# Eight one-row writes of the lead, issued by ScalarE's queue in place of SyncE's

## The chip, the cores and the metric

The kernel runs on one core of a Trainium2 chip. The metric is device time in microseconds (us) of one execution; lower is better. TensorE, VectorE, ScalarE and GpSimd are called PE, DVE, ACT and POOL in the profile, as there; SP is SyncE, which only issues DMAs, and SPq and ACTq are DMA issues by SyncE and ScalarE.

## What is computed

A linear attention with a complex decay (4 batches, 8 heads, 768 positions, 48 dimensions per head), and behind it two feed-forward layers over the 3072 tokens. Cut to what matters, the reference is

```python
mag = np.sqrt(a_re * a_re + a_im * a_im)
scale = np.minimum(mag, 0.999) / (mag + 1e-06)
a_re_n, a_im_n = a_re * scale, a_im * scale
for t in range(S):
    new_re = ar * S_re - ai * S_im
    new_im = ar * S_im + ai * S_re
    S_re, S_im = new_re + kv, new_im              # kv = k[t] outer v[t]
    y[:, :, t] = np.einsum('bhd,bhde->bhe', q[:, :, t], S_re)
h = x @ w_in                                      # x: y as 3072 x 384
sp = np.where(h > 20.0, h, np.log1p(np.exp(np.minimum(h, 20.0))))
x2 = (h * np.tanh(sp)) @ w_out                    # d_ff 2048
out = ((x2 @ w_a) * (x2 @ w_b)) @ w_out2          # d_ff 1536
```

## The kernel before, in words

The 768 positions are cut into 6 chunks of 128, and a chunk of one batch is one unit c (24 of them, `chunk(c)` gives chunk number j and batch b, so units 0 to 3 are the first chunk of the four batches). For a unit the logarithm of the decay's size and its angle are summed over the 128 positions by a matmul with a triangle of ones (`running_sum`, L299). The sum of the logarithms gives two factors, `ep` and `em`, both halves of one tile named `size` (`decay_exp`, L319); the sum of the angles, in turns, is reduced to a fraction of a turn in the tile `a` (`reduce_angle`, L325). `scale_qk` (L356) multiplies q and k by the factors, `trig` (L361) writes cosine and sine, and `rotate_one` (L367) makes from them the rotated `qh` and `kh`, which PE transposes (`transposed`, L376), ScalarE copies out (`transposed_out`, L385) and PE multiplies to scores (`scored_in`, L401). `values` (L416) multiplies the scores with v.

Of each sum the last row (1 x 384 numbers, 1.5 KB) goes on to the next chunk of the same batch by way of memory: `hand_end` (L340) writes the last row of `ep` to `end_d`, and `hand_turn` (L335) the last row of the reduced angle to `turn_d`. `read_end` (L345) reads `end_d` back as the tile `g`, and `carry` (L278) reads `turn_d` for the next chunk.

The first four units are the **lead** (`lead_in`, L796): an order written out by hand as a list of step names (L841), kept on DVE, ACT, PE and POOL by added dependencies (`in_order`, L781), while SyncE's DMAs stand where the program's scheduler puts them. In this list "ep0" to "ep3" are `decay_exp` with `hand_end`, "red0" to "red3" `reduce_angle` with `hand_turn`, "at" the arctangent, "sin" `trig`, "rq" and "rk" the two rotations, "pt" and "pl" the two running sums, and "d1", "d2" the decoding of the first two weight pieces. In the lead `trig` writes cosine and sine into the tile `size` of the same unit, whose first half `hand_end` has to have read by then:

```python
t = st["turn", c]
w = st["turn", c] = st["size", c] if c < B else t
act(out=w[:, 0], in_=t[:, 0], func=AF.Sin, scale=SIN_SCALE)
```

SyncE issues the loads of a, q, k and v (192 KB each) and of the weights (768 KB a piece, `load_weights`, L140). In the built program each DMA takes the next of eight completion counters and is issued only once the DMA that had that counter before has landed.

Behind the lead, block by block of 512 tokens, follow the first layer (`moe1_h`, `mish_factor`, `mish_product`, `moe1_x2`), with the attention of the later chunks in slots between its steps, and then the second layer.

Of the kernel before, what the change touches and what calls it, by code (L numbers as in the profile page):

```python
# [21 lines left out]
def kernel(  # L22
# [14 lines left out]
    nc = tc.nc  # L37
# [31 lines left out]
    C = 128  # L69
# [34 lines left out]
    end_d = [dram.tile([1, H, D], F32, name=f"end_d{b}") for b in range(B)]  # L104
    turn_d = [dram.tile([1, H, D], F32, name=f"turn_d{b}") for b in range(B)]
    good_d = dram.tile([1, P], F32, name="good_d")

    def chunk(c):


        return divmod(c, B)
# [94 lines left out]
    st = {}  # L206
# [128 lines left out]
    def hand_turn(c):  # L335
        j, b = chunk(c)
        if j < NC - 1:
            nc.sync.dma_start(out=turn_d[b], in_=st["turn", c][C - 1:C, 0])

    def hand_end(c):  # L340
        j, b = chunk(c)
        if j < NC - 1:
            nc.sync.dma_start(out=end_d[b], in_=st["ep", c][C - 1:C])

    def read_end(c):  # L345
        j, b = chunk(c)
# [166 lines left out]
    def slot_0(c):  # L513
# [5 lines left out]
        (3, split_ell),  # L519
        (4, carry), (4, split_theta), (4, sum_ell), (5, sum_theta), (5, decay_exp), (6, reduce_angle),  # L520
        (6, hand_turn), (6, hand_end), (7, scale_qk), (10, trig),
    ]
    late = [
# [191 lines left out]
    def judge(pool):  # L715
# [20 lines left out]
        out=csum, in_=csum, pattern=[[1, P]], compare_op=ALU.is_ge, fill=0.0, base=0, channel_multiplier=-1  # L736
# [59 lines left out]
    def lead_in():  # L796
# [20 lines left out]
        def reduced(c):  # L817
            reduce_angle(c)
            hand_turn(c)

        def sizes(c):
            decay_exp(c)
            hand_end(c)
# [93 lines left out]
    for ui in range(len(units) + lag):  # L917
        if ui < len(units):
            b, f = units[ui]
# [202 lines left out]
```

## Time and profile before

| | |
|---|---|
| median of 3 runs | 1114.57 us (1113.7 to 1117.06) |
| profiled execution, its own time | 1116.88 us |
| its span, first to last instruction | 1115.2 us |
| PE, DVE, ACT, POOL busy | 95%, 59%, 55%, 21% of the span |
| mean granted TensorE clock | 0.983 of full speed |
| memory read and written | 72.44 MB and 17.36 MB |

The profile is of one execution. Busy shares are means over stages with different limits, so they tell little of any one stage; the lead takes about the first 62 us of 1115, and its instructions are read one by one in the timeline, where brackets behind a row give the idle time of its engine before it and what ended it.

### The profile page before, as it was taken

Reading aid. Unit: us, or ns where it says so; the run is one execution under the profiler, and the core shown is the slowest. Engines: PE = TensorE matmul, PEld = TensorE weight load, DVE = VectorE, ACT = ScalarE, POOL = GpSimd, SP = SyncE. Lnnn points to the kernel's source line nnn. Section 1 sums busy time; section 2 is a strip of 40 time slices with the busy share of each in tenths; the row PEclk is TensorE's granted clock in tenths of the full one; section 3 lists DMA queues with packets and bytes.
Section 4 is the critical chain, followed back from the end, with each engine's and each line's share of the span. In section 5 each row is a group of like instructions: output and inputs, shape, how many; then the busy total and the mean of one; then the engine's idle time right before and its main releaser. Section 6 shows DMA issues by size and latency. Waiting matters only on the chain.

```text
span 1115.2 us, 15205 instructions
## 1 busy us (share of the span) xinstructions
PE 1062.9 (95%) x5740; PEld 885.4 (79%) x5740; DVE 654.2 (59%) x998; ACT 615.7 (55%) x968; POOL 229.8 (21%) x220
## 2 busy tenths in 40 slices
PE   3799989999999999999999999999999999999997
PEld 1776666787888788878877878888888888888886
DVE  5699975687777677667659999742232322322222
ACT  6769877887888887779766863221121222221211
POOL 2011252444343334333332122200000000000000
PEclk9799999999999999989999999999999999999999
DMA  9445853253344443333226457310010000100000
GB/s 200 77 136 166 210 152 64 63 109 70 82 92 84 90 97 65 65 64 93 65 83 201 133 177 222 121 57 1 14 44 1 29 29 1 43 1 1 29 1 31
DMA packets 203545, 90.87 MB, mean 81 GB/s; under 512 B 144781, under 2 KB 187850, under 8 KB 203466
## 3 DMA queue, kind: packets, MB, share of 16 engines
q1 hardware_dynamic: 202426, 89.64, 32.0%
q8 instruction: 47, 0.77, 0.3%
q10 hardware_dynamic: 1040, 0.20, 0.1%
q14 instruction: 32, 0.26, 0.1%
HBM read 72.44 MB, written 17.36 MB: 81 GB/s over the span
## 4 chain that ended last, share of the span: by engine, by line
PE 56%; ACT 10%; DVE 8%; issue 3%; DMA 2%; POOL 1%; SPq 0%; ACTq 0%; POOLq 0%
PE ops L683 14%; PE psa L658 13%; PE psb L658 13%; PE hps L560 6%; PE x2ps L603 6%; ACT m L59 5%; DVE m L566 1%; DVE kh L370 1%; PE psc L404 1%; ACT L54 1%; PE py L434 1%; DVE m L580 1%; ACT s L59 1%; ACT a L59 1%; ACT r L59 1%
## 5 line engine op out<-in xcount | busy, mean ns | idle before, releaser
L669 DVE TENSOR_TENSOR a_sb<-a_sb,psb 128x512 f32<-128x512 f32 x72 | 49.4, 686 | 224.4 <-PE psb L658 224.4
L59 ACT ACTIVATE m<-m 128x512 f32<-128x512 f32 x192 | 119.4, 627 | 77.3 <-DVE m L566 73.5
L59 ACT ACTIVATE a_sb<-psa 128x512 f32<-128x512 f32 x72 | 43.0, 597 | 162.7 <-PE psa L658 160.6
L59 ACT ACTIVATE ph<-a_sb 128x512 fp32r<-128x512 f32 x72 | 45.4, 631 | 156.0 <-DVE a_sb L669 156.0
L560 PE MATMUL hps<-xh,winh 128*128 128x512 f32 x288 | 120.4, 420 | 6.4 <-DVE gh L577 3.6
L587 POOL TENSOR_TENSOR gl<-m,gh 128x512 fp32r<-128x512 f32 x64 | 83.6, 1306 | 163.0 <-DVE gh L586 152.7
L560 PE MATMUL hps<-xl,winh 128*128 128x512 f32 x288 | 116.3, 404 | 0.7 <-DMA xl<-yt_dl 0.7
L560 PE MATMUL hps<-xh,winl 128*128 128x512 f32 x288 | 114.9, 399 | 0.0
L683 PE MATMUL ops<-woh,ph 128*128 128x384 f32 x288 | 97.1, 337 | 0.0
L683 PE MATMUL ops<-woh,pl 128*128 128x384 f32 x288 | 97.1, 337 | 0.0
L603 PE MATMUL x2ps<-gl,wouth 128*128 128x512 f32 x240 | 94.9, 396 | 2.2 <-DVE gl L587 1.2
L683 PE MATMUL ops<-wol,ph 128*128 128x384 f32 x288 | 96.7, 336 | 0.0
L603 PE MATMUL x2ps<-gh,wouth 128*128 128x512 f32 x240 | 94.1, 405 | 2.3 <-ACT gh L59 1.7
L603 PE MATMUL x2ps<-gh,woutl 128*128 128x512 f32 x240 | 94.1, 392 | 0.0
L658 PE MATMUL psa<-xh,wal 128*128 128x512 f32 x216 | 85.2, 394 | 0.0
L658 PE MATMUL psa<-xl,wah 128*128 128x512 f32 x216 | 85.1, 394 | 0.0
L658 PE MATMUL psa<-xh,wah 128*128 128x512 f32 x216 | 84.4, 391 | 0.0
L658 PE MATMUL psb<-xh,wbh 128*128 128x512 f32 x216 | 84.2, 390 | 0.0
L658 PE MATMUL psb<-xh,wbl 128*128 128x512 f32 x216 | 84.2, 390 | 0.0
L658 PE MATMUL psb<-xl,wbh 128*128 128x512 f32 x216 | 84.2, 390 | 0.0
L566 DVE TENSOR_SCALAR m<-hps 128x512 f32<-128x512 f32 x96 | 65.4, 682 | 20.9 <-PE hps L560 17.5
L580 DVE SCALAR_TENSOR_TENSOR m<-m,hps 128x512 f32<-128x512 f32 x80 | 54.5, 682 | 35.7 <-ACT m L59 35.6
(143 smaller groups left out, 2344.9 us busy)
## 6 DMA issues: line engine op xcount, KB each, us to landing
wraw<-in_moe_w_out_dram SPq DMA_DIRECT2D x14, 768.0 KB
wraw<-in_moe_w_in_dram SPq DMA_DIRECT2D x8, 768.0 KB
a<-in_a_re_dram SPq DMA_DIRECT2D x24, 192.0 KB
q<-in_q_dram SPq DMA_DIRECT2D x24, 192.0 KB
k<-in_k_dram SPq DMA_DIRECT2D x24, 192.0 KB
v<-in_v_dram SPq DMA_DIRECT2D x24, 192.0 KB
wraw<-in_moe_w_a_dram SPq DMA_DIRECT2D x6, 768.0 KB
wraw<-in_moe_w_b_dram SPq DMA_DIRECT2D x6, 768.0 KB
```

Source lines behind the costliest of these rows:

```text
L54: load = nc.scalar.preload_act_table_set(name)
L59: x = nc.scalar.activation(**kw)
L370: eng.tensor_tensor(tile1(c, nm + "h", [P, H, 2, D]), x, w, ALU.mult)
L404: nc.tensor.matmul(p[:, i, :], lhsT=st["kT", c, hf][:, i, :], rhs=st["qT", c, hf][:, i, :], start=True, stop=True)
L560: nc.tensor.matmul(p, lhsT=w[:, kk, :], rhs=x[:, kk, :], start=(i == 0), stop=(i == len(ops) - 1))
L566: nc.vector.tensor_scalar(m, p, 20.0, None, ALU.min)
L580: nc.vector.scalar_tensor_tensor(m, m, 2.5, p, ALU.subtract, ALU.mult)
L587: (nc.vector if on_act else nc.gpsimd).tensor_tensor(gl, m, gh.bitcast(F32), ALU.subtract)
L603: nc.tensor.matmul(x2ps[m], lhsT=w[:, ms], rhs=x, start=(f == 0 and i == 0), stop=(f == NF - 1 and i == len(terms) - 1),)
L658: nc.tensor.matmul(p, lhsT=w[:, kk, :], rhs=x[:, kk, :], start=(i == 0), stop=(i == len(ops) - 1))
L669: nc.vector.tensor_tensor(a_sb, a_sb, pb, ALU.mult)
L683: nc.tensor.matmul(ops_t[t], lhsT=x[:, tsl], rhs=w, start=(f == 0 and i == 0), stop=(f == NF2 - 1 and i == 2),)
```

## The change

In the lead's four units (j = 0) `hand_turn` and `hand_end` issue their DMA from ScalarE's queue in place of SyncE's. The DMAs of later chunks stay where they were.

```diff
     def hand_turn(c):
         j, b = chunk(c)
         if j < NC - 1:
-            nc.sync.dma_start(out=turn_d[b], in_=st["turn", c][C - 1:C, 0])
+            (nc.sync if j else nc.scalar).dma_start(out=turn_d[b], in_=st["turn", c][C - 1:C, 0])
 
     def hand_end(c):
         j, b = chunk(c)
         if j < NC - 1:
-            nc.sync.dma_start(out=end_d[b], in_=st["ep", c][C - 1:C])
+            (nc.sync if j else nc.scalar).dma_start(out=end_d[b], in_=st["ep", c][C - 1:C])
```

DVE, PE and POOL keep their order. On ScalarE, around "ep1", "red1" and "red0" (`end_d_87` belongs to unit 1, `turn_d_91` and `turn_d_90` to units 1 and 0, and the last row is the arctangent of unit 2), the order differs so:

```order
 L59 ACTIVATE size<-pl 128x384 x2
-L59 ACTIVATE r<-s 128x768
+L343 DMA end_d_87<-size 1x384
+L59 ACTIVATE r<-s 128x768
+L338 DMA turn_d_91<-a 1x384
+L338 DMA turn_d_90<-a 1x384
 L54 ACT_TABLE_LOAD
 L59 ACTIVATE a<-a 128x384
```

Three issues stand now ahead of the table load; the two turn rows wait for DVE's `reduce_angle` of units 1 and 0. The row of unit 0, `end_d_86`, stands in the same way behind the exponentials of unit 0, some rows earlier.

On ScalarE behind the arctangent of unit 3, around "ep2", "ep3" and the first copies of the transposed tiles:

```order
-L59 ACTIVATE size<-pl 128x384 x4
-L59 ACTIVATE qT_128<-pqT 96x512
-L59 ACTIVATE kT<-pkT 96x512 x2
+L59 ACTIVATE size<-pl 128x384 x2
+L343 DMA end_d_88<-size 1x384
+L59 ACTIVATE size<-pl 128x384 x2
+L343 DMA end_d_89<-size 1x384
+L59 ACTIVATE qT_128<-pqT 96x512
+L59 ACTIVATE kT<-pkT 96x512
+L338 DMA turn_d_92<-a 1x384
+L338 DMA turn_d_93<-a 1x384
+L59 ACTIVATE kT<-pkT 96x512
```

Two issues stand between and behind the four exponentials, and two, which wait for `reduce_angle` of units 2 and 3, between the first and the second copy of a transposed k.

On SyncE, behind the load of the second piece of w_in:

```order
 L151 DMA wraw<-in_moe_w_in_dram 128x3x512
-L343 DMA end_d_86<-size 1x384
-L343 DMA end_d_87<-size 1x384
-L338 DMA turn_d_91<-a 1x384
-L338 DMA turn_d_90<-a 1x384
-L351 DMA g<-end_d_86 48x8x1 x2
-L351 DMA g<-end_d_87 48x8x1 x2
-L216 DMA a<-in_a_re_dram 128x8x48
-L216 DMA a<-in_a_im_dram 128x8x48
```

The eight writes are gone from here, and the eight reads of `g` stand together ahead of the two loads of a. The eight counters are dealt anew up to that point: SyncE's load of v for unit 0 waits now for `end_d_86`, that of the first piece of w_out for `end_d_87`, and the two loads of a for unit 4 for `turn_d_91` and `turn_d_90`. From the load of q for unit 4 on, order and counters are the same.

## Rows read from the trace of the kernel before

**Rows 1.** The page: the chain that ended last, shares of the span by engine

```profile
PE 56%; ACT 10%; DVE 8%; issue 3%; DMA 2%; POOL 1%; SPq 0%; ACTq 0%; POOLq 0%
```

**Rows 2.** Timeline of ScalarE: start us, us, engine, line, operation, out<-in, count, idle before

```profile
18.72 0.85 ACT L59 ACTIVATE size<-pl 128x384 f32<-128x384 f32 x2
...
20.32 1.28 ACT L54 ACT_TABLE_LOAD   x1
21.62 0.52 ACT L59 ACTIVATE a<-a 128x384 f32<-128x384 f32 x1
32.88 0.52 ACT L59 ACTIVATE size<-a 128x384 f32<-128x384 f32 x1 [10.74 <-DMA end_d<-size]
...
36.55 1.64 ACT L59 ACTIVATE size<-pl 128x384 f32<-128x384 f32 x4
...
39.92 0.59 ACT L59 ACTIVATE kT<-pkT 96x512 f32<-96x512 f32 x1 [0.19 <-PE pkT L382]
```

**Rows 3.** Timeline of SyncE's issues, 18 to 41 us

```profile
18.53 4.18 SPq L235 DMA_DIRECT2D v<-in_v_dram  x4
...
24.89 3.80 SPq L151 DMA_DIRECT2D wraw<-in_moe_w_in_dram  x1
28.79 0.66 SPq L343 DMA_DIRECT2D end_d<-size  x2
...
32.81 1.86 SPq L351 DMA_DIRECT2D g<-end_d  x4
```

**Rows 4.** Timeline of DVE, 20 to 60 us

```profile
20.79 0.56 DVE L330 TENSOR_TENSOR a<-pt,a 128x384 f32<-128x384 f32 x1
...
22.13 0.55 DVE L359 TENSOR_TENSOR k<-k,size 128x384 f32<-128x384 f32 x1
...
33.94 0.96 DVE L370 TENSOR_TENSOR qh<-q,size 128x768 f32<-128x768 f32 x1 [9.93 <-ACT size L59]
...
39.46 0.56 DVE L330 TENSOR_TENSOR a<-pt,a 128x384 f32<-128x384 f32 x1
...
57.43 0.54 DVE L165 TENSOR_SCALAR wout<-wraw 128x768 uint32<-128x768 uint32 x1
```

**Rows 5.** Timeline of PE, 22 to 47 us

```profile
22.19 1.27 PE L305 MATMUL pt<-a,tsum 128*128 128x384 f32 x2 [2.27 <-ACT a L59]
23.60 1.65 PE L305 MATMUL pl<-size,csum 128*128 128x384 f32 x2
35.04 1.06 PE L382 MATMUL pqT<-ident,qh 128*96 128x128 f32 x4 [9.80 <-DVE qh L370]
...
45.04 1.88 PE L425 MATMUL pyt<-v,am 128*128 128x48 f32 x16
```

**Rows 6.** Table by windows: window, us, busy of each engine, PEclk, DMA share, GB/s

```profile
0.00:19.50 19.50, 6.35 (x10) 2.80 (x10) 10.46 (x25) 14.85 (x21) 5.62 (x23) 1.00 1.11 190
...
0.00:32.80 32.80, 9.68 (x14) 3.60 (x14) 14.83 (x34) 17.46 (x23) 5.62 (x23) 0.84 1.06 204
```

**Rows 7.** DMA issues: ScalarE's first, what waited for it, and SyncE's one-row writes

```profile
0.81 0.47 ACTq L216 DMA_DIRECT2D a<-in_a_im_dram  x1
...
4.98 0.84 ACT L59 ACTIVATE s<-a 128x768 f32<-128x768 f32 x1 [2.38 <-DMA a<-in_a_im_dram]
...
L343 SPq DMA_DIRECT2D end_d<-size x20: 233/254/1312, 28.8 to 438.4; - x20
...
L338 SPq DMA_DIRECT2D turn_d<-a x20: 214/253/663, 29.5 to 441.5; - x20
```

**Rows 8.** Table by windows: the granted clock around PE's idle stretch

```profile
24.00:33.00 9.00, 1.25 (x2) 0.10 (x1) 0.01 (x1) 0.12 (x1) 0.00 (x0) 0.50 0.90 238
...
36.00:40.00 4.00, 4.00 (x18) 3.11 (x18) 3.90 (x7) 3.33 (x8) 0.00 (x0) 0.54 0.52 99
40.00:45.00 5.00, 5.00 (x47) 5.00 (x46) 4.36 (x9) 4.97 (x9) 0.00 (x0) 1.00 0.59 87
```

**Rows 9.** Table by windows behind the lead, and SyncE's own waits from 20 to 72 us

```profile
90.00:120.00 30.00, 30.00 (x173) 21.32 (x172) 28.76 (x45) 27.90 (x46) 7.52 (x5) 0.99 0.74 184
120.00:150.00 30.00, 27.68 (x154) 19.95 (x154) 29.90 (x35) 23.24 (x36) 15.23 (x9) 0.94 0.58 146
...
SPq L151 <- DVE wout L167: 16.7, 2, 16.2
```

## The prediction

> **What bounds the kernel now.** I read the page's chain first: PE holds 56% of it [rows 1], nearly all behind the lead, in work that the change leaves alone. So the question is when that work begins. The change touches the first 45 us, so I read the timelines of ScalarE, SyncE, DVE and PE there one beside the other, to find where all of them stand still.
>
> They do once. ScalarE ends the arctangent of unit 2 at 22.14 us (21.62 + 0.52) and then waits 10.74 us, until 32.88, for the DMA `end_d<-size` [rows 2]. The waiting instruction is the cosine of unit 0: it overwrites the tile `size` from which the one-row write still has to read. DVE then idles 9.93 us and PE 9.80 us, each for the engine ahead of it [rows 4, 5]; no other engine covers the stretch.
>
> Why is the row late? It was ready early: the `ep` and `em` of unit 1 were made at 18.72 to 19.57 [rows 2], those of unit 0 five us before. SyncE issues the two rows only at 28.79, behind the loads of v and a weight load whose issue took 3.80 us [rows 3]. And once issued they stand behind SyncE's bytes: ahead of them SyncE and ScalarE have issued 22 loads of 192 KB (eight of a, eight of q and k, four of v, two of a for unit 4) and three weight pieces of 768 KB, 6.68 MB. The window up to 32.80 moved 32.80 x 204 GB/s = 6.69 MB [rows 6]. So the cosine starts when the last byte ahead of the rows has moved, which is what one queue served in order would give.
>
> **The change part by part**, against the profiled execution's 1116.88 us (1115.2 span and 1.7 around it; it lies 2.3 above the median of 1114.57, so I work out a difference and take it from the median).
>
> *The end rows of units 0 and 1 go early.* They are issued from ScalarE right behind their exponentials, about 14.4 and 19.5 us. When do they land? At worst they share one order with SyncE's bytes. By 19.5 SyncE has issued loads up to the first of v, 4.13 MB in all, and 19.50 x 190 = 3.71 MB have moved [rows 6]; the 0.42 MB left take 2.2 us, so 21.7. Another bound is ScalarE's own DMA at the start: 192 KB, issued at 0.81, waited for until 4.98, 4.2 us beside SyncE's loads [rows 7]; that would be 23.7 for unit 1 and 18.6 for unit 0. I take 22 for unit 1. Either way the rows are no longer what ends the wait.
>
> A rule speaks against this gain. The Trainium skill, "DMA: Bandwidth & Descriptors", section "Issuing engines are not separate DMA queues", says that DMAs started by different engines run on the same 16 DMA engines, so that starting them from several engines saves only the sequencer's time to start them. By it the sum would be eight issues, two us or less. The row on the byte count says that here being in front of 2.5 MB is the gain, shared engines or not.
>
> *What is late next.* ScalarE has to issue `turn_d_91` and `turn_d_90` ahead of its table load. The second needs the reduced angle of unit 0, ready at 20.79 + 0.56 = 21.35 [rows 4]. An issue costs 0.25 us, the median of SyncE's 20 writes of each kind [rows 7]; no such write on ScalarE is in the trace. Bounds: nothing (it hides behind a running activation) and 0.47, ScalarE's one issue of a far larger load. I take 0.25, the same transfer. So the table load starts at 21.60 in place of 20.32, a cost of 1.28 us, taken from the stall; the arctangent starts at 22.90 and the cosine of unit 0 at about 23.35. It also needs DVE to have read `size`: done at 22.13 + 0.55 = 22.68 [rows 4]. Gain at this point: 32.88 - 23.35 = **9.5 us**. The cosine of unit 1 follows at 24.3, behind 22 and behind 23.7. The end rows of units 0 and 1 themselves cost ScalarE at most 0.25 each, and what follows them waits for DVE and PE work with slack; I take nothing, 0.5 at the upper end.
>
> *Issues behind the stall.* `end_d_88` and `end_d_89` stand among the four exponentials, which run without a gap [rows 2]: 2 x 0.25 = **0.5 us** lost. `turn_d_92` and `turn_d_93` stand ahead of the second copy of a transposed k. That began at 39.92; the angle of unit 3 was ready at 39.46 + 0.56 = 40.02 [rows 4]. Both shift alike, so the wait and one issue cost 0.10 + 0.25 = **0.35 us**. What is queued behind it are the copies for the scores, for which PE and then DVE wait, so I count it whole.
>
> *PE.* The sum of angles of unit 2 needs the arctangent, so it moves from 22.19 to 23.42; with the sum behind it (22.19 to 25.25, 3.06 us) PE is free at 26.5, whereas the first transpose would want 35.04 - 9.5 = 25.5 [rows 5]: up to **0.9 us** late. Against that stands the clock: the granted clock was 0.50 (the 1.2 GHz level) over the idle stretch and still 0.54 from 36 to 40, then 1.00 [rows 8]. With hardly any idle stretch it should come back earlier in the work. At full speed the PE work of 36 to 40 would take up to 1.9 us less; at the least nothing. I take the middle, 0.9, and the two cancel.
>
> *SyncE.* Its loads of v wait for `end_d_86`, of w_out for `end_d_87`. Even some us late this costs nothing: the first matmul with v stands at 45.04 [rows 5], so about 36 now, and the v bytes are through by 4.72 MB, some 25 us; the decode of w_out stands at 57.43, now 48 [rows 4], and its load ends by 28. The reads of `g`, 32.81 before [rows 3], now stand together ahead of the loads of a for unit 5, at some 33 us; `g` is used behind the lead.
>
> *Does the rest move along?* From 90 to 150 us DVE is busy 28.76 and 29.90 of 30 us, and SyncE waited for DVE's decode before it could load the next weights, once for 16.2 us [rows 9]. So the next stage is paced by DVE, whose order is unchanged and simply starts earlier; no transfer holds an absolute date there.
>
> **Sum**: 9.5 - 0.5 - 0.35 - 0.9 + 0.9 = 8.65. Profiled time 1108.3, median **1106.0 us**.
>
> Ends: the whole 10.74 goes and the clock gives 1.9 more with no price: 12.6 faster, 1102. All eight issues on the path at 0.47 (3.8), the wait for the angle of unit 0 (21.35 - 20.32 = 1.0), 0.1 and 0.9: 10.74 - 5.8 = 4.9 faster, 1109.7.
>
> **Rivals.** *(1) Part of it is given back behind the lead*, because weight loads, 184 GB/s there [rows 9], hold some of it. If half is kept: 1110.3. For it: DMA share 0.74. Against: SyncE waits for DVE, not DVE for SyncE. *(2) Only starting time is saved.* The rows on ScalarE's queue still land when SyncE's backlog is through, and the gain is eight issues of 0.25: 1112.6. The trace's one transfer on ScalarE's queue, landed after 4.2 us beside SyncE's loads, speaks against it. The Trainium skill's section on issuing engines, named above, would speak for it. *(3) The change doesn't do what it says*: another reader of `size` or a counter holds the cosine at 32.9, and the time stays 1114.6. DVE's last reading ends at 22.68, and no other DMA reads that tile. *(4) Slower: ScalarE pays for issues.* SyncE's issues run up to 1.31 us for the same row and 3.80 for a weight piece [rows 3, 7]; take it that ScalarE cannot compute meanwhile. At 1.8 us each, eight cost 14.4, and with the waits of 1.0 and 0.1 the kernel is 4.8 slower: 1119.4. It turns slower than the bound below from (10.74 - 1.1 + 3.3)/8 = 1.6 us an issue. Against: ScalarE's own issue took 0.47 with many more packets, and its queue is empty where SyncE's was full.
>
> **How the numbers follow.** About 0.3% (3.3 us) is what a measurement of this kernel can tell from no change. Forecast 0.86; rival 1 0.06, half of it beyond the bound; rival 2 0.03; rival 3 0.02; rival 4 0.03. Faster 0.86 + 0.03 = 0.89, same 0.03 + 0.03 + 0.02 = 0.08, slower 0.03. Range: the forecast's ends without their last us at the lower side, where every price would have to be nothing, and up to rival 1's time: 1103.0 to 1110.5.
>
> **What would show it.** ScalarE's wait of 10.74 on `end_d` gone, the cosine at 23 to 24 us; an idle time of about 1 us ahead of the table load at 21.6; DVE's and PE's idle of 9.9 and 9.8 shrunk to about 1; the decode of w_out at about 49 in place of 57.43 [rows 4]; from there every row about 8.6 us earlier, to a span of some 1106.6. It is wrong if the cosine still waits for a DMA, if ACTq rows take over 0.5 us, or if the shift is there at the end of the lead and not at 150.

## The result, and the profile after

The change runs in 1105.85 us (median of 4 runs, 1104.91 to 1106.71), beside 1115.18 us for four runs of the kernel before: a ratio of 0.9915, 95% interval 0.9897 to 0.9933, 9.3 us faster. The forecast was 1106.0. The profiled execution took 1105.91 us, its span is 1104.2 us, 11.0 below the span of before.

ScalarE's timeline of the change around the former wait, to be held against [rows 2]:

```profile
14.11 0.48 ACTq L343 DMA_DIRECT2D end_d<-size  x1
...
19.41 0.22 ACTq L343 DMA_DIRECT2D end_d<-size  x1
19.68 0.84 ACT L59 ACTIVATE r<-s 128x768 f32<-128x768 f32 x1
20.32 1.68 ACTq L338 DMA_DIRECT2D turn_d<-a  x2
22.03 1.28 ACT L54 ACT_TABLE_LOAD   x1 [1.51 <-DVE a L330]
23.32 0.52 ACT L59 ACTIVATE a<-a 128x384 f32<-128x384 f32 x1
23.75 0.51 ACT L59 ACTIVATE size<-a 128x384 f32<-128x384 f32 x1
...
29.04 0.59 ACT L59 ACTIVATE qT<-pqT 96x512 f32<-96x512 f32 x1
...
29.53 0.58 ACT L59 ACTIVATE kT<-pkT 96x512 f32<-96x512 f32 x1
30.91 0.24 ACTq L338 DMA_DIRECT2D turn_d<-a  x1
31.19 0.59 ACT L59 ACTIVATE kT<-pkT 96x512 f32<-96x512 f32 x1 [1.07 <-PE pkT L382]
```

The wait of 10.74 us on `end_d` is gone: the cosine of unit 0 starts at 23.75 in place of 32.88, right behind the arctangent. A new wait of 1.51 us stands ahead of the table load, and it is the second turn row, which waits for DVE. The last row needs care. It puts 1.07 us of idle time down to PE, but the row above it says who held ScalarE: the turn row of unit 3 was issued only at 30.91, when DVE had just made its angle, and the copy stood behind it in ScalarE's queue.

SyncE's issues [rows 3], DVE [rows 4] and PE [rows 5] of the change at the same places:

```profile
18.91 3.99 SPq L235 DMA_DIRECT2D v<-in_v_dram  x4
...
25.14 3.88 SPq L151 DMA_DIRECT2D wraw<-in_moe_w_in_dram  x1
29.33 5.46 SPq L351 DMA_DIRECT2D g<-end_d  x8
34.90 0.41 SPq L216 DMA_DIRECT2D a<-in_a_re_dram  x1
```

```profile
14.41 0.56 DVE L165 TENSOR_SCALAR wf<-wraw 128x768 uint32<-128x768 uint32 x1 [1.37 <-DMA wraw<-in_moe_w_in_dram]
...
21.18 0.56 DVE L330 TENSOR_TENSOR a<-pt,a 128x384 f32<-128x384 f32 x1
...
24.80 0.96 DVE L370 TENSOR_TENSOR qh<-q,size 128x768 f32<-128x768 f32 x1 [0.39 <-ACT size L59]
...
30.32 0.56 DVE L330 TENSOR_TENSOR a<-pt,a 128x384 f32<-128x384 f32 x1
...
49.13 0.54 DVE L165 TENSOR_SCALAR wout<-wraw 128x768 uint32<-128x768 uint32 x1
```

```profile
23.90 1.65 PE L305 MATMUL pt<-a,tsum 128*128 128x384 f32 x2 [3.24 <-ACT a L59]
25.34 1.49 PE L305 MATMUL pl<-size,csum 128*128 128x384 f32 x2
26.62 0.95 PE L382 MATMUL pqT<-ident,qh 128*96 128x128 f32 x4
```

DVE waits 0.39 us for the cosine in place of 9.93, and PE's first transposes start at 26.62 without the idle 9.80. The loads of v and of the second piece of w_in stand within 0.4 us of where they stood, so the rows that moved cost SyncE nothing there. The decode of w_out, which the text below takes as the end of the lead, moved from 57.43 to 49.13: 8.30 us.

The granted clock in two windows of [rows 8], and the busy times in the first window of [rows 9]:

```profile
24.00:33.00 9.00, 8.23 (x44) 5.85 (x45) 8.47 (x15) 7.90 (x16) 0.00 (x0) 0.82 0.98 242
...
36.00:40.00 4.00, 4.00 (x39) 4.00 (x38) 3.92 (x5) 2.10 (x6) 0.00 (x0) 1.00 0.91 168
...
90.00:120.00 30.00, 30.00 (x200) 21.60 (x199) 29.83 (x45) 26.40 (x41) 6.92 (x5) 1.00 0.72 190
```

PE is busy for most of 24 to 33 us at a mean granted clock of 0.82, where it was mostly idle at 0.50 before.

### The profile page after: what moved, and what is told of

It is laid out like the page before. It is cut to its first block, busy times and chain, and to the rows that moved or that the text cites. A ratio compares the mean times of both kernels' runs of the same rounds, so it can differ in the third digit from the quotient of the medians.

```text
span 1104.2 us, 15205 instructions
## 1 busy us (share of the span) xinstructions
PE 1061.1 (96%) x5740; PEld 884.0 (80%) x5740; DVE 657.6 (60%) x998; ACT 615.2 (56%) x968; POOL 229.0 (21%) x220
## 4 chain that ended last, share of the span: by engine, by line
PE 49%; ACT 11%; DVE 10%; issue 5%; DMA 3%; POOL 1%; SPq 0%; ACTq 0%; DVEq 0%; POOLq 0%
PE ops L683 12%; PE psb L658 12%; PE psa L658 12%; ACT m L59 6%; PE hps L560 5%; PE x2ps L603 5%; DVE m L566 2%; DVE kh L370 1%; ACT L54 1%; DVE m L580 1%; ACT a L59 1%; ACT s L59 1%; PE psc L404 1%; PE py L434 1%; DMA good_d<-good 1%
```

## The experiments

The theory (A): the end rows of units 0 and 1 land early because they stand ahead of some 2.5 MB or more of SyncE's loads, the cosine needs them, and that is the whole gain; the other six rows only cost. The rivals: a queue of its own makes the row fast (B), SyncE freed of issues is what counts (C), something else that moved gave the gain (D), a DMA takes a fixed time whatever stands ahead of it (E), and ScalarE's issues lie beside other work and cost nothing (F).

**Which rows carry the gain.** Only the end rows on ScalarE's queue:

```diff
-            (nc.sync if j else nc.scalar).dma_start(out=turn_d[b], in_=st["turn", c][C - 1:C, 0])
+            nc.sync.dma_start(out=turn_d[b], in_=st["turn", c][C - 1:C, 0])
```

> Only the four end rows go by ScalarE's queue; the turn rows are SyncE's again. Theory A (the gain is the early landing of the end rows of units 0 and 1, which the cosine waits for; the turn rows only cost): ScalarE's wait of 10.7 us is gone, the table load stands at about 20.5 in place of 22.0 and the cosine, now held by the arctangent and by DVE's last reading of size, at 22.7 to 23.0 in place of 23.75; the decode of w_out at about 48.0 in place of 49.1; time about 1104.8 us, 1 us below the change. Rival C (SyncE freed of eight issues is what counts): only half of the gain, about 1110 us.

Measured: 1103.32 us beside 1112.53, a ratio of 0.9906 (0.9882 to 0.9930). The cosine stands at 22.16, the decode of w_out at 46.58, some 0.5 and 1.4 us earlier than expected:

```profile
22.16 0.51 ACT L59 ACTIVATE size<-a 128x384 f32<-128x384 f32 x1
```

Only the turn rows there:

```diff
-            (nc.sync if j else nc.scalar).dma_start(out=end_d[b], in_=st["ep", c][C - 1:C])
+            nc.sync.dma_start(out=end_d[b], in_=st["ep", c][C - 1:C])
```

> Only the four turn rows go by ScalarE's queue; the end rows are SyncE's again. Theory A: the cosine still waits for the end row until about 32.9; ScalarE's wait of 1.5 us for DVE and the two issues at 20 to 22 us lie inside that wait and cost nothing; later 0.35 us; time 1115 to 1116 us, no gain. Rival C (SyncE freed): a part of the gain, about 1110 us.

Measured: 1114.04 us beside 1112.53, a ratio of 1.0009 (0.9991 to 1.0027). ScalarE's timeline has the new wait and the old one, and behind them the wait of the turn rows of units 2 and 3:

```profile
20.92 1.28 ACT L54 ACT_TABLE_LOAD   x1 [0.72 <-DVE a L330]
22.21 0.52 ACT L59 ACTIVATE a<-a 128x384 f32<-128x384 f32 x1
32.84 0.52 ACT L59 ACTIVATE size<-a 128x384 f32<-128x384 f32 x1 [10.10 <-DMA end_d<-size]
...
39.15 1.08 ACTq L338 DMA_DIRECT2D turn_d<-a  x2
40.28 0.59 ACT L59 ACTIVATE kT<-pkT 96x512 f32<-96x512 f32 x1 [0.59 <-DVE a L330]
```

The end rows carry the gain alone. The 0.72 us lie inside the wait for the row. SyncE freed of four issues gains nothing, which speaks against C; the next two kernels, in which SyncE issues all eight rows, settle it.

**The queue, or the place in the order.** Nothing on ScalarE's queue; SyncE's own order puts the end rows first. `loads()` holds the loads of v, w_out, the next a and w_in, which stood ahead of the lead's list (cut to the step that calls it):

```diff
...
         def sizes(c):
             decay_exp(c)
             hand_end(c)
+            if c == 1:
+                loads()
```

> Nothing on ScalarE's queue; SyncE issues the end rows of units 0 and 1 ahead of the loads of v, w_out, the next a and w_in, and no engine but SyncE has another order. Theory A (place in the order counts, not the queue): SyncE waits some 0.7 us for the exponentials of unit 1, issues the rows at 19.3 to 20.2, they land by 22 to 23.5; the cosine stands at 22.7 to 23.8; time 1104 to 1106 us. Rival B (a queue of its own is what makes the row fast): the rows land as late as SyncE's bytes around them, the cosine stands well behind 25, and the time lies at 1110 to 1115 us.

Measured: 1102.10 us beside 1112.53, a ratio of 0.9896 (0.9871 to 0.9921), 2 us below the time that I had expected. SyncE's issues and ScalarE's timeline:

```profile
18.03 1.39 SPq L343 DMA_DIRECT2D end_d<-size  x2
19.47 2.70 SPq L235 DMA_DIRECT2D v<-in_v_dram  x4
22.21 1.13 SPq L151 DMA_DIRECT2D wraw<-in_moe_w_out_dram  x1
```

```profile
21.58 0.52 ACT L59 ACTIVATE a<-a 128x384 f32<-128x384 f32 x1
22.01 0.51 ACT L59 ACTIVATE size<-a 128x384 f32<-128x384 f32 x1
...
32.93 0.52 ACT L59 ACTIVATE size<-a 128x384 f32<-128x384 f32 x1 [0.44 <-DMA end_d<-size]
```

The gain is there on SyncE's queue too, so no queue of its own is needed for it (B falls), and SyncE need not be freed of the issues (C falls): the date of the row counts. The third row shows the end row of unit 2, which is still late here and costs 0.44 us.

The other side of the same wait: the rows stay late on SyncE, but the cosine no longer needs them, because GpSimd copies them first into a tile that is not used yet. The copies are rounded to fp32r, a rounded form of fp32. The tile `xl` is made earlier for it (cut):

```diff
+            if c < 2:
+                if 0 not in xl_t:
+                    xl_t[0] = xp.tile([P, KM, TN], F32R, tag="xl", name="xl")
+                row = xl_t[0][96:, c, :H * D].rearrange("p (h d) -> p h d", d=D)
+                nc.gpsimd.tensor_scalar(row, st["ep", c][96:], 1.0, 0.0, ALU.mult, ALU.add)
+                nc.sync.dma_start(out=end_d[b], in_=row[31:32].bitcast(F32))
+                return
             nc.sync.dma_start(out=end_d[b], in_=st["ep", c][C - 1:C])
...
```

> All rows are SyncE's and as late as before, but GpSimd first copies the end rows of units 0 and 1 into a tile that is not used yet, so the cosine waits for that copy and not for the DMA. The copies are rounded to fp32r, which is a small change of the computation. Theory A (the wait for the reading of size is all that the late row costs): the cosine stands at 22.7 to 23.3, the end rows are still issued behind 28 us, time 1104.5 to 1106 us. Rival D (something else that the change moved, SyncE's order or the eight completion counters, gave the gain): no gain, or less than half, 1110 us and above.

Measured: 1103.93 us beside 1112.53, a ratio of 0.9911 (0.9885 to 0.9938); the cosine at 21.98, 0.7 us earlier than expected, while SyncE issues the rows as late as before:

```profile
21.98 0.51 ACT L59 ACTIVATE size<-a 128x384 f32<-128x384 f32 x1
```

```profile
28.18 0.66 SPq L350 DMA_DIRECT2D end_d<-xl  x2
```

So neither SyncE's order nor the counters gave the gain (D falls). The late row cost only by the tile that it still had to read.

**When a row lands.** SyncE's early rows once more, but behind the four loads of v (4.72 MB ahead of them), and then behind the load of w_out too (5.50 MB). The edit is that of the early rows, with `load_v`, or `load_v` and the load of w_out, left ahead of the list; the first of the two, cut:

```diff
+        late_loads = {}
         for c in range(B):
             load_v(c)
...
+        def loads():
+            late_loads["d2"] = steps1[1]()[0]
+            run_to(slot[0] + 1)
+            late_loads["w"] = steps1[2]()
...
```

> Nothing on ScalarE's queue; SyncE issues the end rows of units 0 and 1 behind the four loads of v and ahead of w_out, so 4.72 MB stand ahead of them. Theory A (the row lands when the bytes ahead of it in SyncE's order have moved): at 195 to 200 GB/s that is 23.6 to 24.2 us, and the cosine of unit 0 starts at 24 to 24.8, 1.9 to 2.7 us later than with the rows ahead of v. Rival E (a fixed 3.5 to 4 us from issue to landing): issued at 22.2, landed at about 26, the cosine at 26.

> As the run before, but with the rows behind the load of w_out too: 5.50 MB ahead of them. Theory A: at 200 to 202 GB/s 27.3 to 27.6 us, the cosine of unit 0 at 27.3 to 28, some 3.3 us later than with the rows behind v alone, and 5 us earlier than before; time about 5 us below the kernel before. Rival E (fixed time from issue to landing): issued 0.9 us later than in the run before, so the cosine only 0.9 us later than there.

Measured: 1106.34 and 1107.89 us beside 1111.90, ratios of 0.9946 (0.9930 to 0.9963) and 0.9962 (0.9947 to 0.9976); the second is 4.0 us faster than before where 5 were expected. SyncE's issue and ScalarE's wait, behind v and behind w_out:

```profile
22.41 0.74 SPq L343 DMA_DIRECT2D end_d<-size  x2
```

```profile
25.12 0.52 ACT L59 ACTIVATE size<-a 128x384 f32<-128x384 f32 x1 [2.97 <-DMA end_d<-size]
```

```profile
23.23 0.64 SPq L343 DMA_DIRECT2D end_d<-size  x2
```

```profile
27.75 0.52 ACT L59 ACTIVATE size<-a 128x384 f32<-128x384 f32 x1 [5.73 <-DMA end_d<-size]
```

SyncE issued the two pairs at 22.41 and 23.23, 0.8 us apart, and the waits end 2.63 us apart, so no fixed time explains them (E falls). The windows up to the two dates bear the count of bytes out within some 5%:

```profile
0.00:25.10 25.10, 9.26 (x14) 3.73 (x14) 14.85 (x34) 17.45 (x23) 5.63 (x23) 0.95 1.24 192
```

```profile
0.00:27.70 27.70, 9.23 (x14) 3.65 (x14) 14.84 (x34) 17.45 (x23) 5.61 (x23) 0.91 1.24 208
```

25.10 x 192 is 4.82 MB for 4.72, and 27.70 x 208 is 5.76 for 5.50. The first cosine came 0.3 us later than the latest date I had expected. With 6.68 MB ahead, before, the same wait ended at 32.88 [rows 2].

The traces also hold every DMA packet with its queue, start and size, and a row is one packet of 1536 bytes. So each row's packet can be set beside the bytes of the loads whose issue had ended when the row's began, and beside the bytes of loads that had moved when the packet started:

| kernel, row, queue | row issued at | MB issued before it | its packet at | MB moved by then |
|---|---|---|---|---|
| before, end row of unit 0, SyncE's | 28.79 | 6.68 | 32.20 | 6.63 |
| early rows, the same, SyncE's | 18.03 | 3.93 | 20.23 | 3.89 |
| behind v, the same, SyncE's | 22.41 | 4.72 | 24.19 | 4.68 |
| behind w_out, the same, SyncE's | 23.23 | 5.51 | 26.92 | 5.54 |
| the change, end row of unit 1, ScalarE's | 19.41 | 3.93 | 20.76 | 3.88 |
| the change, turn row of unit 2, ScalarE's | 29.45 | 6.68 | 32.21 | 6.51 |
| all end rows alone, unit 2, ScalarE's | 26.34 | 5.90 | 28.41 | 5.87 |

In the four rows of SyncE's queue the count fits within 0.05 MB. On ScalarE's queue the rows do not pass the loads that SyncE had issued before them either, but for some 0.2 MB. So what counts is when a row is issued, and not by which engine; this is the strongest evidence against B.

**The price of the other six rows.** The change and the kernel with only the end rows of units 0 and 1 on ScalarE's queue, on one chip:

```diff
-            (nc.sync if j else nc.scalar).dma_start(out=end_d[b], in_=st["ep", c][C - 1:C])
+            (nc.scalar if c < 2 else nc.sync).dma_start(out=end_d[b], in_=st["ep", c][C - 1:C])
```

with the turn rows SyncE's again as above.

> The change itself, on the same chip as the next run. Against the kernel before: a ratio of 0.990 to 0.993; the cosine at 23.6 to 23.9 us and the decode of w_out at about 49.1 as in its first profile.

> Only the end rows of units 0 and 1 go by ScalarE's queue; those of units 2 and 3 and all turn rows are SyncE's. Theory A (two of the eight issues carry the gain, the other six only cost): the cosine at about 22.1 us, the four exponentials without a gap at 25.7 to 27.4, the decode of w_out at 46.0 to 46.6, 2.5 to 3 us ahead of the change; time 2 to 3 us below the change on the same chip, a ratio of about 0.9975 between the two. If units 2 and 3 come to wait for their end rows, behind the load of w_in, their cosine stands at 33 in place of 32.3 and 0.5 us of it is lost. Rival F (ScalarE's six issues lie beside other work): the same decode time as the change within 0.5 us.

Measured: 1104.37 and 1101.52 us beside 1111.90, ratios of 0.9940 (0.9919 to 0.9960) and 0.9898 (0.9881 to 0.9915). The cosine at 22.52 and 22.23, the decode of w_out at 47.89 and 45.84. The change's ratio and its cosine lie outside what I had expected for its second run: the cosine of the same kernel is 1.23 us earlier than in its first profile.

Then four on another chip: the change, SyncE's early rows, the end rows of units 0 and 1 on ScalarE's queue, and SyncE's early rows with the four turn rows on ScalarE's queue.

> The change itself, on the same chip as the next three. A ratio of 0.991 to 0.994 to the kernel before. The cosine stands at 0.3 us or more behind that of the end-rows-01 kernel, and the further behind, the later the first piece of w_in lands: two issues on ScalarE wait for DVE, which decodes that piece first.

> The kernel with SyncE's end rows of units 0 and 1 ahead of v again, nothing on ScalarE's queue: the cosine at 22.0, the decode of w_out at about 46.1, 1.8 to 3 us ahead of the change; time 2 to 3 us below the change.

> The kernel with only the end rows of units 0 and 1 on ScalarE's queue again: the cosine at 22.2, the decode of w_out at about 45.9; the same time as the kernel with SyncE's early rows, within 1 us, so that it is the date of the row and not its queue that counts; 2 to 3 us below the change.

> SyncE's early end rows, and in addition all four turn rows on ScalarE's queue. Against the kernel with early rows alone this shows the price of the turn rows by themselves. Theory A: ScalarE waits for the reduced angles of units 0 and 1 ahead of its table load (0.4 us or more) and of units 2 and 3 ahead of the second copy of a transposed k (0.7 us or more); the decode of w_out 1.2 to 2.5 us later than with early rows alone, and the time 1 to 2.5 us longer. Rival F (ScalarE's issues lie beside other work): the same decode time within 0.5 us.

Measured, in this order: 1104.45, 1101.97, 1101.66 and 1103.40 us beside 1113.87; ratios of 0.9919 (0.9900 to 0.9939), 0.9899 (0.9881 to 0.9917), 0.9901 (0.9881 to 0.9920) and 0.9907 (0.9890 to 0.9924). ScalarE's timeline with early rows and turn rows:

```profile
20.90 1.28 ACT L54 ACT_TABLE_LOAD   x1 [0.64 <-DVE a L330]
...
29.20 0.80 ACTq L338 DMA_DIRECT2D turn_d<-a  x2
30.05 0.59 ACT L59 ACTIVATE kT<-pkT 96x512 f32<-96x512 f32 x1 [0.32 <-PE pqT L382]
```

The traces side by side: start of the cosine of unit 0, start of the decode of w_out, the time between, and the mean granted clock over the ten us from the cosine on (1.00 is the 2.4 GHz level, 0.50 the 1.2 GHz level, and a mean between them mixes the two):

| kernel | cosine | decode | between | clock |
|---|---|---|---|---|
| before | 32.88 | 57.43 | 24.55 | 0.66 |
| the change, three profiles | 23.75, 22.52, 23.11 | 49.13, 47.89, 48.49 | 25.38, 25.37, 25.38 | 0.83, 0.75, 1.00 |
| turn rows alone | 32.84 | 58.22 | 25.38 | 0.61 |
| all end rows alone | 22.16 | 46.58 | 24.42 | 0.83 |
| end rows of units 0 and 1, two profiles | 22.23, 22.16 | 45.84, 45.83 | 23.61, 23.67 | 1.00, 1.00 |
| SyncE's early rows, two profiles | 22.01, 21.96 | 46.06, 45.57 | 24.05, 23.61 | 0.83, 1.00 |
| SyncE's early rows, turn rows on ScalarE | 22.63 | 47.58 | 24.95 | 1.00 |
| rows copied by GpSimd | 21.98 | 46.58 | 24.60 | 1.00 |
| SyncE's rows behind v, behind w_out | 25.12, 27.75 | 50.19, 51.55 | 25.07, 23.80 | 0.61, 0.74 |

The turn rows alone delay the end of the lead by 2.0 us (47.58 against 45.57, both at a clock of 1.00): 0.67 at the cosine, 1.34 behind it. Against 46.06, the other profile of SyncE's early rows, in which the end row of unit 2 cost 0.44, it is 1.5. So F falls in the trace. In whole times, the kernels without the six other rows on ScalarE are 2.5 to 2.9 us faster than the change on the same chip. Between the change and the end rows of units 0 and 1 the intervals part on the first of the two chips, 0.9919 against 0.9915, and overlap on the second; the price of the turn rows by themselves, 1.4 us between two medians, is within the intervals. SyncE's early rows and the two end rows on ScalarE's queue are alike, and both beat the change by their medians.

## Why the prediction was right

*In all: 8.65 us forecast, 9.33 measured*, and 7.5 and 9.4 in the two later measurements of the same two kernels. The wait and what removes it were right. That 1106.0 (1114.57 - 8.65 is 1105.92) met 1105.85 so closely is luck.

*The bound.* Right. One wait in the lead, for a row whose tile is needed, held ScalarE, DVE and PE one behind the other; with the rows alone moved, or copied away, it is gone.

*The gain at the cosine: 9.5 forecast, 9.13 in the profile.* The table load came at 22.03 in place of 21.60, because the first piece of w_in landed 0.38 us later in this execution (its decode began at 14.41, before at 14.03), and DVE's angles with it. One sentence of that step was misread: the DVE row that I gave as the last reading of unit 0's `size`, ending at 22.68 [rows 4], is that of unit 1: in the lead's list "sc1" stands behind "red0". Unit 0's ends earlier. It bound nothing, but it made me expect the cosine of the experiments at 22.7 to 23.0, and it came at 22.0 to 22.2, as soon as the arctangent was done.

*The landing date.* I bounded it at 21.7 to 23.7 for unit 1, and nothing waited for it in the change. Its packet moved at 20.76 in this profile and at up to 21.55 in the others with that row on ScalarE's queue. On SyncE's queue the waits ended 0.7 to 0.9 us behind the packet, so it landed at about 21.5 to 22.4, an estimate. The picture behind the lower bound, one order with SyncE's bytes, is what the packets show: a row moves when the loads issued before it have moved, on SyncE's queue and, within 0.2 MB, on ScalarE's. The Trainium skill's rule from "DMA: Bandwidth & Descriptors", section "Issuing engines are not separate DMA queues", that another engine saves only the time to start a DMA, would have given two us. The runs agree with the rule in that ScalarE's queue is no faster than a place ahead of v in SyncE's (0.9901 and 0.9899). The two us I had worked out from eight issues, and they left out that an earlier issue also comes ahead of some 2.5 MB, which is where the measured 9.3 us come from.

*The costs behind the cosine: 0.85 forecast, 0.83 measured* (25.38 - 24.55). The sum held by luck, while its terms did not. The turn rows of units 2 and 3 I put at 0.35. Moved alone, they move the second copy of a transposed k from 7.04 to 7.44 us behind the cosine (40.28 - 32.84), 0.40, and the end of the lead by 0.83, which is the whole cost. The kernel with the turn rows alone has no end rows on ScalarE and a clock of 0.61; the change has the end rows and a late PE at clocks of 0.75 to 1.00; the time between is 25.37 or 25.38 in all four profiles, and the second copy stands 7.42 to 7.44 behind the cosine. There ScalarE waits for DVE's angle of unit 3, so three terms of the sum do not show in the change: the 0.5 for the issues of the end rows of units 2 and 3 (the first copy behind them came 0.12 later, 29.04 - 23.75 against 38.05 - 32.88), the 0.9 for PE, which was late as forecast (26.62, forecast 26.5), and the 0.9 for the clock. This is the row of before:

```profile
38.05 0.61 ACT L59 ACTIVATE qT<-pqT 96x512 f32<-96x512 f32 x1
```

In the kernels with early rows the same copy stands 6.11 and 6.12 us behind the cosine without the turn rows and 7.42 with them (30.05 - 22.63), as it is 7.44 in the change (31.19 - 23.75). DVE's angle holds it there, while PE would deliver the transposed k sooner than before. So the mis-sized term is this wait, 1.3 us for 0.35 once the stall is gone, because I shifted the copy and the angle alike. What the clock gives shows where ScalarE has no turn rows: 25.07, 24.55 and 23.80 us between at 0.61, 0.66 and 0.74, and 23.6 to 23.7 in three of four profiles at 1.00. They differ in more than the clock, so no run prices it by itself. From the copy to the decode the four profiles with 25.37 or 25.38 take 0.4 us longer than before, and why stays open.

*SyncE.* Right: the four loads that now wait for ScalarE's rows (one of v, one of w_out, two of a) stand within 0.4 us of where they stood.

*The rest moves along.* Right, but the reason that I gave is not shown. From 90 to 120 us I read DVE's 28.76 busy us as what paces that stage, but in the same line PE is busy for all 30.00 [rows 9]; which of the two paces it, no run shows. The first store of the first layer moved by 7.9 us, as in the rows below of before and of the change, and the gain was not given back:

```profile
L614 SPq DMA_DIRECT2D x_d<-x2o x18: 319/343/970, 191.5 to 663.1; - x18
```

```profile
L614 SPq DMA_DIRECT2D x_d<-x2o x18: 320/343/531, 183.6 to 652.0; - x18
```

The 3.2 us more that lie between the last stores (663.1 and 652.0) need not be the change's: with the turn rows alone on ScalarE, where nothing is gained, the two dates are 192.2 and 661.8, so 2 us of them are there without any gain in the lead. What the rest is, no run shows.

*The rivals.* Rival 1 (given back later), rival 3 (something else holds the cosine) and rival 4 (ScalarE pays for its issues) did not come: issues of 0.22 to 0.48 us in the change's profiles, never near 1.6. Rival 2 (the rows still land when SyncE's backlog is through) had the mechanism right and the price wrong: at 19.41 us that backlog was 0.3 MB, 3.93 issued and 3.63 moved, where at 28.79 it was 0.9. What ScalarE does pay is not the issue but the wait in front of it.

## What to carry to other kernels

A small transfer can hold a whole chain by the tile that it still has to read, and its date is set by the bytes that were issued before it, here by either engine: look for a wait on a tiny DMA behind large loads, and issue it ahead of them, from SyncE or ScalarE, or copy the row away. Move only the rows that something waits for. A DMA on ScalarE's queue cost little here by its issue (0.22 to 0.48 us), but whatever it waits for, everything behind it on that engine waits for as well.

## What was not expected

The change ties ScalarE to the landing of a weight piece that it does not read. In its three profiles DVE starts to decode the first piece of w_in at 14.41, 13.19 and 13.78, and the cosine follows at 23.75, 22.52 and 23.11: 9.34, 9.33 and 9.33 us behind it each time. The piece comes first in DVE's fixed order, the angles of units 1 and 0 behind it, and ScalarE's turn rows wait for those. SyncE's early rows with the turn rows on ScalarE give 13.28 and 22.63, 9.35 us, as well. With the turn rows on SyncE the cosine stood at 21.96 to 22.23, 8.7 to 8.9 us behind the start of that decode, in every profile with the end rows ahead of v or copied away.
